# A linear-attention and token-mixing block: the whole last product by seven block products instead of three quarters of it, the first product in other groups

## The chip, the cores and the metric

One core of one Trainium2 chip. The metric is the time of one execution in microseconds of device time; the median of several runs is given. A separate execution is taken with the hardware profiler, and its trace shows when each engine worked and on what.

## What is computed

The input is a prompt of S = 2048 tokens with D = 448 channels. A linear attention block and then a token-mixing MLP, both with adaptive layer norm from a condition vector, are added to it. The change lies in the second half:

```python
def _B_ref(x, w1, b1, w2, b2):
    h = _layernorm(x, axis=-1)                     # (B, S, D)
    u = jnp.einsum("bsd,sf->bdf", h, w1) + b1      # (B, D, F), F = 1792
    u = _gelu(u)
    y = jnp.einsum("bdf,fs->bds", u, w2) + b2      # (B, D, S)
    return y transposed to (B, S, D)

x = x + ga * _A_ref(h, A_wqkv, A_wo)
h = _layernorm(x, axis=-1) * (1 + cb) + sb
x = x + gb * _B_ref(h, B_w1, B_b1, B_w2, B_b2)
```

So there are two large products. The *first product* is u = w1ᵀ h: for each of 14 blocks of 128 values of f, a sum over 16 tiles of 128 tokens. The *last product* is y = w2ᵀ u: for each of 16 tiles of 128 tokens, a sum over the 14 blocks of f. All arrays are float32.

## The kernel before

**Precision.** A float32 operand is cut in two parts of the format `fp32r`: ScalarE copies it (the high part), VectorE subtracts that from it (the low part). `split` (lines 78 to 80) does both. A product of two operands is then three matmuls, high by high, high by low and low by high. `acc3` (lines 833 to 836) issues these three, each with 128 stationary columns and 448 moving ones, into one PSUM bank.

**The first product.** w1 is read in *pieces*, each one token tile by a group of n blocks of f. `W1G` (line 291) has the groups: f 0 to 3, 4 to 7, 8 to 11 and then 12 and 13, so there are 64 pieces, of 512 columns or, in the last group, of 256. `load_to` issues their loads on SP's queue, `split_to` cuts them, `step` multiplies a piece with the normalised tokens `H2h`, `H2l` into n banks `up`. A group goes over all 16 token tiles, and then its n banks hold finished sums. Part of the first 20 pieces' work runs under the attention; from about 230 us on TensorE does nothing but the first product. In the loop over groups, each step also does: loads eight pieces ahead (`AHEAD`), cuts three ahead, one *job* out of a list, and at every second step one of the 16 x rows (the residual, to which the bias is added on VectorE, and which is then written to `out`, or to a parking place in DRAM for tiles 12 to 15).

**u and its parts.** `finish_u` (line 936) gives the jobs for one block f: gelu on ScalarE and a multiplication by the gate on VectorE; `cut`, the cut of the whole 448-wide u into `uw`, which holds the high part of both channel halves and then the low part of both; and, at each odd f, four sums and differences of the halves (`sums`) and their cuts `ut` (`parts4`).

**The last product by block products.** Two token tiles by two neighbouring blocks of f form a 2x2 block matrix a11, a12, a21, a22 of w2, and the two blocks of u, cut in two channel halves of 224, form another, b11 to b22. Seven products instead of eight then do, after Winograd's form of Strassen's scheme (`PRODS`, line 1005, gives for each of the seven the factor from w2, the factor from u, the bank it adds to, and the sum computed for a later one):

```python
    PRODS = (("a11", "b11", 0, None), ("a12", "b21", 1, ("s2", "s1", "a11")),
             ("s2", "t2", 0, ("s3", "a22", "s2", ALU.subtract, "a11")),
             ("s1", "t1", 2, ("s4", "a12", "s2", ALU.subtract, "a12")), ("s3", "t3", 0, None),
             ("s4", "b22", 2, None), ("a22", "t4", 0, None))
```

They are numbered m = 0 to 6; `q` numbers the pair of token tiles. `mult7` issues a product: for each of the seven pairs of f (`PAIRS`) one matmul of 448 moving columns, the high part of the factor from w2 by high and low part of the factor from u, and one of 224, its low part by the high part. For b11, b21 and b22 the moving operand is taken out of `uw`: 224 columns from the high part and 224 from the low part, which there lie 448 apart. For t1 to t4 both lie next to each other. `load_quads` loads the four blocks for all f in two DMAs each (four pairs of f, then three), and GpSimd's DMA adds a22 to a21, which makes s1. `split7` cuts one factor and computes the sum that `PRODS` names. `out7` takes a bank out: copies on ScalarE after m = 0, 2 and 3, sums on VectorE after m = 1, 4 and 5 (`out2`, two instructions each), both after m = 6. A finished tile `yt` is added to `out` in DRAM by GpSimd's DMA (`add_to_x`).

**The rest of the last product.** Token tiles 0 to 11 go this way (`NS7` = 6 pairs). Tiles 12 to 15 go the plain way: `load1`, `split1`, `mult1` with `acc3`, one *item* per f (two tiles at once for 12 and 13). The list `order` begins with eight plain items, mixes the others between the block products and ends with ten. The last two f of tile 15 are multiplied by `mult_last` in two halves of 224 columns, so that the first half is added and stored while the second is multiplied.

**What sets the order.** The order on every engine is that of the program: each engine's queue is strictly in turn, and there is no scheduler. A tile of SBUF comes from the pool `slots` (74 of 2 KB per partition); a new one waits until the one that had its place was read for the last time. SP's queue issues the plain loads and stores, GpSimd's the adding ones. Loads are issued 12 entries of `order` ahead (`LOAD2`), cuts four ahead (`SPLIT2`).

Of the kernel before, what the change touches and what calls it, by code (L numbers as in the profile page):

```python
# [33 lines left out]
AHEAD = 8  # L34
LAG = 5
LAST, CUT = 2, 224
# [11 lines left out]
def block_kernel(ctx: ExitStack, tc: tile.TileContext, x, xt, wqkv, wo, w1, b1, w2, b2, c, wmod, wfirst, out):  # L48
# [242 lines left out]
    W1G = [(0, 4), (4, 4), (8, 4), (12, 2)]  # L291
    pieces = [(w1, t, f0, n) for f0, n in W1G for t in range(NT)]
# [3 lines left out]
    def load_to(i):  # L296
        while done["load"] < min(i, len(pieces)):
            k = done["load"]
            src, r, c0, n = pieces[k]
            raws[k] = slot(f"pr{k}", n * P)  # L300
            nc.sync.dma_start(raws[k], src[r * P:(r + 1) * P, c0 * P:(c0 + n) * P])
            done["load"] += 1

    def split_to(i):
        while done["split"] < min(i, len(pieces)):
            k = done["split"]
            n = pieces[k][3]
            if k in TOKP:
                hi, lo = tslot(f"ph{k}", F32R, w=n * P), tslot(f"pl{k}", F32R, w=n * P)
            else:  # L310
                hi, lo = slot(f"ph{k}", n * P, F32R), slot(f"pl{k}", n * P, F32R)
# [526 lines left out]
    def step(k, accs, mh, ml, first, last):  # L838
        hi, lo = parts.pop(k)
        for i, ps in enumerate(accs):  # L840
            acc3(ps, hi, lo, slice(i * P, (i + 1) * P), mh, ml, first, last)
# [14 lines left out]
    for i in range(NT + LAG):  # L856
# [15 lines left out]
        if t >= 0:  # L872
            if t == 0:
                accs = [bank(f"up{f}") for f in range(4)]
            if i > NT:
                if not early:
                    early = [bank(f"up{W1G[1][0] + f}") for f in range(W1G[1][1])]
                r = i - NT - 1
                step(NT + r, early, H2h[r], H2l[r], r == 0, False)
            step(t, accs, H2h[t], H2l[t], t == 0, t == NT - 1)  # L880
# [55 lines left out]
    def finish_u(f, ps):  # L936
# [7 lines left out]
        def cut():  # L944
            uw[f] = uparts.tile([P, 4 * HD], F32R, name=f"uw{f}")
            split(ufull[f], uw[f][:, :D], uw[f][:, D:])
            w = uw[f].rearrange("p (x d) -> p x d", x=2)
            left, right = ((w[:, :, h:h + HD], w[:, 0, h:h + HD]) for h in (0, HD))
            if f % 2:
                uops["b21", r], uops["b22", r] = left, right  # L950
            else:
                uops["b11", r] = left
# [9 lines left out]
        def parts4(key, half, name):  # L962
            return lambda: u_parts(r, name, ufull[key][:, half * HD:(half + 1) * HD])
# [50 lines left out]
    def mult7(q, m):  # L1014
        a, b, k, _ = PRODS[m]
        opens = m in (0, 1, 3)
# [3 lines left out]
        closes = m in (1, 5, 6)  # L1020
        cut = hilo.pop((q, m))
        for r in range(PAIRS):
# [28 lines left out]
    def out7(q, m):  # L1051
# [20 lines left out]

    def load1(t, n, f):
        raw2[t, f] = slot(f"q{t}_{f}", n * P)
        nc.sync.dma_start(raw2[t, f], w2[f * P:(f + 1) * P, t * P:(t + n) * P])

    def split1(t, n, f):
        w = slot(f"qw{t}_{f}", 2 * n * P, F32R)
        hilo[t, n, f] = (w[:, :n * P], w[:, n * P:])
        split(raw2.pop((t, f)), *hilo[t, n, f])  # L1080

    def mult1(t, n, f):
        if f == 0:
            for i in range(n):
                acc2[t + i] = bank(f"yp{t + i}")
        hi, lo = hilo.pop((t, n, f))
        for i in range(n):
            acc3(acc2[t + i], hi, lo, slice(i * P, (i + 1) * P), uw[f][:, :D], uw[f][:, D:], f == 0,
                 f == NF - 1 - (LAST if t == NT - 1 else 0))


    def mult_last(t):
        nc.vector.tensor_add(X[t], acc2[t][:, :D], X[t])
        for c0, c1 in ((0, CUT), (CUT, D)):
            ps = bank(f"yl{c0}")[:, :c1 - c0]
            n = 0
            for f in range(NF - LAST, NF):
                wh, wl = hilo[t, 1, f]
                a, b = uw[f][:, c0:c1], uw[f][:, D + c0:D + c1]
                for w, m in ((wh, a), (wh, b), (wl, a)):  # L1100
                    nc.tensor.matmul(ps, w, m, start=n == 0, stop=n == 3 * LAST - 1)
                    n += 1
            x = X[t][:, c0:c1]
            nc.vector.tensor_add(x, ps, x)
            nc.sync.dma_start(of[t * P:(t + 1) * P, c0:c1], x)

    def out1(t, n, f):
        if f < NF - 1:
            return
        for i in range(t, t + n):  # L1110
            nc.vector.tensor_add(X[i], acc2[i][:, :D], X[i])
            store(i)


    sevens = [(q, m) for q in range(NS7) for m in range(7)]
    plains = [(t, n, f) for t, n in ((12, 2), (14, 1), (15, 1)) for f in range(NF)]
    LEAD, TAIL = 8, 10
# [152 lines left out]
```

## Time and profile before

| | us |
|---|---|
| median of 3 runs | 447.32 |
| lowest and highest | 446.92, 447.51 |
| the profiled execution | 448.35 |
| its span | 446.2 |

The span is the time from the first to the last recorded event of the profiled execution; the execution's own time has another 2.15 us around it. The page of the profile has the span in 40 slices. These are its rows for TensorE (PE), VectorE (DVE), ScalarE (ACT) and GpSimd (POOL); each digit is a slice's busy share in tenths:

```profile
PE   7999999999999999999999999999999999999997
PEld 6878899999899999989999999999999999999996
DVE  3989997689998899896477776649688787978873
ACT  3899877748656876667664345336554546356531
POOL 3227563300025355554300000000110211302101
```

A slice is 11.2 us. The first product alone has slices 21 to 28, the last product 29 to 40. In the last product the fourth row (ScalarE) stands at about half, the third (VectorE) at seven to nine tenths. In the rows of groups that the prediction shows, a line begins with the line of the code, the engine and the operation, then output and inputs by the program's names and their shapes; a row of a timeline begins with start and duration in us, and ends in brackets with the idle time before it and what ended it.

### The profile page before, as it was taken

What the parts mean: (1) busy time and instruction counts of PE and PEld (TensorE: products, weight loads), DVE (VectorE), ACT (ScalarE), POOL (GpSimd) and SP (SyncE); (2) the same over time, 40 slices, a digit from 0 to 9 for tenths busy, and PEclk for the clock granted to TensorE, in tenths of its full rate; (3) what the DMA queues carried; (4) which work ended last, traced back from release to release, by engine and by line L of the source; (5) the groups of instructions that cost most, each with busy time, mean ns of one, the idle gap of its engine ahead of it and who ended that gap; (6) DMA issues with size and microseconds to landing.
All of it is one profiled execution on the core that took longest, in us unless ns stands there. A gap on an engine that the chain in (4) does not pass through costs nothing.

```text
span 446.2 us, 7331 instructions
## 1 busy us (share of the span) xinstructions
PE 439.1 (98%) x2370; PEld 405.5 (91%) x2370; DVE 353.5 (79%) x801; ACT 267.5 (60%) x580; POOL 104.3 (23%) x188
## 2 busy tenths in 40 slices
PE   7999999999999999999999999999999999999997
PEld 6878899999899999989999999999999999999996
DVE  3989997689998899896477776649688787978873
ACT  3899877748656876667664345336554546356531
POOL 3227563300025355554300000000110211302101
PEclk9999999999999999999999999999999999999999
DMA  7997999545100004222416453227987569966334
GB/s 236 378 303 165 215 241 229 104 147 181 54 0 1 24 25 114 54 48 47 143 54 217 137 178 127 90 88 228 257 201 194 92 177 214 208 183 110 54 89 62
DMA packets 58853, 63.22 MB, mean 142 GB/s; under 512 B 5248, under 2 KB 49344, under 8 KB 58816
## 3 DMA queue, kind: packets, MB, share of 16 engines
q1 hardware_dynamic: 51616, 51.17, 38.0%
q0 software_dynamic: 7200, 11.60, 16.4%
q8 instruction: 18, 0.29, 0.3%
q14 instruction: 19, 0.16, 0.1%
HBM read 46.57 MB, written 7.34 MB: 121 GB/s over the span
## 4 chain that ended last, share of the span: by engine, by line
PE 91%; ACT 3%; DVE 2%; POOL 1%; DMA 1%; issue 1%; SPq 0%; ACTq 0%
PE y L1026 14%; PE up L836 10%; PE up L835 10%; PE up L834 9%; PE cacc L512 7%; PE qp L418 7%; PE op L783 7%; PE y L1027 7%; PE kp L418 6%; PE yp L834 2%; PE yp L836 2%; PE yp L835 2%; PE tq L767 1%; DMA xt<-in_xt_dram 1%; PE qp L425 1%
## 5 line engine op out<-in xcount | busy, mean ns | idle before, releaser
L836 PE MATMUL up<-h2h,pl 128*128 128x448 f32 x224 | 81.4, 363 | 0.0
L835 PE MATMUL up<-h2l,ph 128*128 128x448 f32 x224 | 81.2, 362 | 0.0
L834 PE MATMUL up<-h2h,ph 128*128 128x448 f32 x224 | 80.8, 361 | 0.0
L80 DVE TENSOR_TENSOR pl<-pr,ph 128x512 fp32r<-128x512 f32 (+1 forms) x60 | 36.3, 616 | 14.2 <-ACT ph L79 9.9
L79 ACT ACTIVATE ph<-pr 128x512 fp32r<-128x512 f32 (+1 forms) x60 | 33.0, 570 | 24.0 <-PE up L835 17.7
L835 PEld LDWEIGHTS up<-h2l,ph 128*128 128x128 f32 x224 | 42.1, 188 | 3.1
L834 PEld LDWEIGHTS up<-h2h,ph 128*128 128x128 f32 x224 | 41.9, 187 | 3.0
L836 PEld LDWEIGHTS up<-h2h,pl 128*128 128x128 f32 x224 | 42.1, 188 | 2.4
L988 POOL DMA_DIRECT2D a<-a x12 | 10.9, 952 | 113.8 <-DMA a<-in_B_w_dram 101.7
L1046 POOL DMA_DIRECT2D out_dram<-yt x12 | 10.5, 874 | 82.3 <-DVE yt L1037 53.9
L512 PE MATMUL cacc<-pkh,xh 128*128 128x448 f32 x64 | 24.4, 381 | 0.3 <-ACT pkh L486 0.3
L783 PE MATMUL op<-wph,pth 112*128 112x448 f32 x64 | 24.5, 382 | 0.0
L418 PE MATMUL kp<-wh,hh 128*128 128x448 f32 x64 | 23.2, 373 | 1.1 <-ACT wh L253 1.1
L1032 ACT ACTIVATE cc<-y 128x448 f32<-128x448 f32 x18 | 9.8, 545 | 23.4 <-PE y L1027 20.4
L512 PE MATMUL cacc<-pkl,xh 128*128 128x448 f32 x64 | 23.3, 364 | 0.2 <-DVE pkl L488 0.2
L418 PE MATMUL qp<-wh,hh 128*128 128x448 f32 x64 | 23.3, 364 | 0.0
L783 PE MATMUL op<-wpl,pth 112*128 112x448 f32 x64 | 23.2, 363 | 0.0
L783 PE MATMUL op<-wph,ptl 112*128 112x448 f32 x64 | 23.2, 362 | 0.0
L834 PE MATMUL yp<-uw,qw 128*128 128x448 f32 x54 | 19.9, 368 | 0.0
L771 ACT ACTIVATE pth<-tq 112x512 fp32r<-112x512 f32 x16 | 9.6, 599 | 17.1 <-PE tq L767 17.1
L836 PE MATMUL yp<-uw,qw 128*128 128x448 f32 x54 | 19.7, 364 | 0.0
L835 PE MATMUL yp<-uw,qw 128*128 128x448 f32 x54 | 19.6, 364 | 0.0
(241 smaller groups left out, 1308.9 us busy)
## 6 DMA issues: line engine op xcount, KB each, us to landing
pr<-in_B_w_dram SPq DMA_DIRECT2D x48, 256.0 KB, 3.0
a<-in_B_w_dram SPq DMA_DIRECT2D x24, 256.0 KB, 4.9
a<-in_B_w_dram SPq DMA_DIRECT2D x24, 192.0 KB, 4.9
xt<-in_xt_dram SPq DMA_DIRECT2D x16, 256.0 KB, 4.9
x<-in_A_x_dram SPq DMA_DIRECT2D x16, 224.0 KB, 4.9
wm<-in_B_wmod_dram SPq DMA_DIRECT2D x16, 196.0 KB, 5.1
wr<-in_qkv_dram SPq DMA_DIRECT2D x12, 224.0 KB, 5.3
out_dram<-x SPq DMA_DIRECT2D x12, 224.0 KB, 2.0
```

Source lines behind the costliest of these rows:

```text
L79: nc.scalar.activation(hi, full, AF.Copy)
L80: nc.vector.tensor_sub(lo, full, hi.bitcast(F32))
L418: nc.tensor.matmul(pps[t, j][:, :D], a[:, ch * P:(ch + 1) * P], w, start=first, stop=False)
L512: nc.tensor.matmul(cacc[ch][:, :D], a[:, s], b, start=(t == 0 and i == 0), stop=(t == NT - 1 and i == len(todo) - 1))
L783: nc.tensor.matmul(opb[t][:, :D], a[:, s], b, start=(n == 0), stop=(n == 11))
L834: nc.tensor.matmul(ps[:, :D], hi[:, sl], mh, start=first, stop=False)
L835: nc.tensor.matmul(ps[:, :D], hi[:, sl], ml, start=False, stop=False)
L836: nc.tensor.matmul(ps[:, :D], lo[:, sl], mh, start=False, stop=last)
L988: nc.gpsimd.dma_start(w, a, accum_op=ALU.add)
L1026: nc.tensor.matmul(ps[:, :D], h[:, s], w, start=opens and r == 0, stop=False, skip_group_check=True)
L1027: nc.tensor.matmul(ps[:, :HD], l[:, s], wh, start=False, stop=closes and r == PAIRS - 1, skip_group_check=True)
L1046: nc.gpsimd.dma_start(of[t * P:(t + 1) * P, :], ysum.pop(t), accum_op=ALU.add)
```

## The change

1. `NS7` is `NT // 2` = 8: all 16 token tiles go by block products. `load1`, `split1`, `mult1`, `out1`, `mult_last` and the mixed `order` go.
2. Every half of u that is a factor gets a tile of its own with high and low part next to each other: b11 of an even f, b21 and b22 of an odd one. The right half of an even f is no longer cut. These tiles, and the sums' cuts of the last two pairs of f (`UT_APART`), come from `uparts` instead of `slots`.
3. `mult7` takes a range of pairs. Five products are begun with six of the seven pairs (`BEGUN`), (q, m) = (0,0), (0,1), (0,3), (1,0), (1,1); then each gets its seventh; then the other products of q = 0 and 1 follow, mixed, and from q = 2 on m = 0 to 6 in turn.
4. `W1G` has groups of 4, 4, 2, 2 and 2 f. A piece of the groups of 2 f is two token tiles by two f, so that every piece has 512 columns and there are 56. `AHEAD` is 8 for the groups of four and `NEAR` = 5 for those of two; cuts are three or two ahead.
5. The x rows go at every step instead of every second one; all but tile 15 are written to `out` at once. `add_to_x` then serves 15 tiles.
6. Tile 15 is held in SBUF at the end (`fetch_x`) and is added to and stored in two halves by `finish`.
7. `PRE2` says after which token tiles of the last group loads and cuts for the last product are issued: five factors with their sums are cut there. `JOBS` and `CUT2` do the same for the first entries of `order`.

```diff
+AHEAD, NEAR = 8, 5
+PRE2 = ((0, (1, 0)), (6, (1, 1)), (8, (4, 2)), (12, (4, 3)), (14, (4, 4)), (15, (4, 5)))
+JOBS = {0: 2, 1: 2}
+UT_APART = 5
+CUT2 = {2: 9, 3: 9, 4: 8, 5: 7}
...
-    W1G = [(0, 4), (4, 4), (8, 4), (12, 2)]
-    pieces = [(w1, t, f0, n) for f0, n in W1G for t in range(NT)]
+    W1G = [(0, 4), (4, 4), (8, 2), (10, 2), (12, 2)]
+    pieces = [(t, 4 // n, f0, n) for f0, n in W1G for t in range(0, NT, 4 // n)]
+    place = {(f0, t + i): (k, i * n * P) for k, (t, m, f0, n) in enumerate(pieces) for i in range(m)}
...
-    NS7 = 6
-    uw, uops, ufull = {}, {}, {}
+    NS7 = NT // 2
+    uops, ufull = {}, {}
 
     def u_parts(r, name, src):
-        w = slot(f"u{name}_{r}", dt=F32R)
+        if name[0] == "b" or r >= UT_APART:
+            w = uparts.tile([P, D], F32R, name=f"u{name}_{r}")
+        else:
+            w = slot(f"u{name}_{r}", dt=F32R)
         split(src, w[:, :HD], w[:, HD:])
         uops[name, r] = (w, w[:, :HD])
...
-        def cut():
-            uw[f] = uparts.tile([P, 4 * HD], F32R, name=f"uw{f}")
-            split(ufull[f], uw[f][:, :D], uw[f][:, D:])
-            w = uw[f].rearrange("p (x d) -> p x d", x=2)
-            left, right = ((w[:, :, h:h + HD], w[:, 0, h:h + HD]) for h in (0, HD))
...
+        def part(key, half, name):
+            return lambda: u_parts(r, name, ufull[key][:, half * HD:(half + 1) * HD])
...
         if f % 2 == 0:
-            return [act, cut]
+            return [act, part(f, 0, "b11")]
         two = lambda p, q: lambda: (p(), q())
-        return [act, cut, sums, two(parts4(("a", r), 1, "t2"), parts4(("a", r), 0, "t1")),
-                two(parts4(("b", r), 0, "t3"), parts4(("b", r), 1, "t4"))]
+        return [act, two(part(f, 0, "b21"), part(f, 1, "b22")), sums,
+                two(part(("a", r), 1, "t2"), part(("a", r), 0, "t1")),
+                two(part(("b", r), 0, "t3"), part(("b", r), 1, "t4"))]
...
-    def mult7(q, m):
+    def mult7(q, m, r0, r1):
         a, b, k, _ = PRODS[m]
-        opens = m in (0, 1, 3)
+        opens = m in (0, 1, 3) and r0 == 0
...
-        closes = m in (1, 5, 6)
-        cut = hilo.pop((q, m))
-        for r in range(PAIRS):
+        closes = m in (1, 5, 6) and r1 == PAIRS
+        cut = hilo[q, m]
+        for r in range(r0, r1):
...
             out2(q, 0, "c5", t1, 1)
+            if q == NS7 - 1:
+                finish(t1, HD, yt(t1)[:, HD:])
         elif m == 5:
             out2(q, 2, "c2", t0, 1)
             add_to_x(t0)
+        elif q == NS7 - 1:
+            x = X[t1][:, :HD]
+            nc.vector.tensor_add(x, acc2[q, 0][:, :HD], x)
+            finish(t1, 0, acc2[q, 0][:, HD:D])
...
+    def finish(t, c0, y):
+        x = X[t][:, c0:c0 + HD]
+        nc.vector.tensor_add(x, y, x)
+        nc.sync.dma_start(of[t * P:(t + 1) * P, c0:c0 + HD], x)
...
+    FIRST = ((0, 0), (0, 1), (0, 3), (1, 0), (1, 1))
+    BEGUN = PAIRS - 1
+    order = [(q, m, 0, BEGUN) for q, m in FIRST]
+    order += [(q, m, BEGUN, PAIRS) for q, m in ((0, 0), (1, 0), (0, 1), (1, 1), (0, 3))]
+    order += [(q, m, 0, PAIRS) for q, m in ((0, 2), (1, 3), (0, 4), (0, 5), (1, 2), (0, 6), (1, 4), (1, 5), (1, 6))]
+    order += [(q, m, 0, PAIRS) for q in range(2, NS7) for m in range(7)]
...
-            load_to(k + AHEAD)
-            split_to(k + 3)
+            k = place[o0, r][0]
+            load_to(k + (AHEAD if n == 4 else NEAR))
+            split_to(k + (3 if n == 4 else 2))
             if jobs:
                 jobs.pop(0)()
-            if xleft and k % 2:
+            if xleft:
...
+            if o0 + n == NF:
+                for at, (load, cut) in PRE2:
+                    if at == r:
+                        load2(load)
+                        split2(cut)
```

More of the change, by code (lines that the diff above doesn't have):

```diff
@@ L1092, in mult_last @@
[L1092 to L1117, printed above, removed]
-    order = [("p", p) for p in plains[:LEAD]]
-    mid = plains[LEAD:len(plains) - TAIL]
-    for i, p in enumerate(sevens):
-        order.append(("s", p))
-        order += [("p", x) for x in mid[i * len(mid) // len(sevens):(i + 1) * len(mid) // len(sevens)]]
@@ L1133, in load2 @@
         while cnt["load"] < min(n, len(order)):
-            kind, p = order[cnt["load"]]
-            if kind == "p":
-                load1(*p)
-            elif p[1] == 0:
-                load_quads(p[0])
+            q, m, r0, _ = order[cnt["load"]]
+            if m == 0 and r0 == 0:
+                load_quads(q)
             cnt["load"] += 1
@@ L1145, in block_kernel @@
     xleft = list(range(NT))
-    xpark = {t: park.tile([P, D], F32, name=f"xpark{t}") for t in range(2 * NS7, NT)}
+    xpark = {t: park.tile([P, D], F32, name=f"xpark{t}") for t in range(NT - 1, NT)}
     stored = []
```

99 lines of the change are left out of this document (33 added, 66 removed).

## The prediction

> **What bounds the kernel now.** I read the page first (share of the span per engine), then what TensorE waited for, then the stretches by stage, then the order of time inside the last product.
>
> ```profile
> PE 439.1 (98%) x2370; PEld 405.5 (91%) x2370; DVE 353.5 (79%) x801; ACT 267.5 (60%) x580; POOL 104.3 (23%) x188
> ```
>
> TensorE (PE) is busy 98% of the span. Its waits are seven rows, of which these are the first and the last:
>
> ```profile
> PE warm L178 <- DVE roots L101: 1.1, 1, 1.1
> ...
> PE cacc L512 <- DVE pkl L488: 0.2, 1, 0.2
> ```
>
> Together the seven make 3.6 us, and none of them names `up`, `y` or `yp`, the tiles of the two products that the change touches. So there TensorE's own work is the time. The stretches say the same; the columns are length, then busy time of PE, weight load, VectorE (DVE), ScalarE (ACT), GpSimd (POOL), clock, DMA share and GB/s:
>
> ```profile
> 230.00:316.10 86.10, 86.10 (x433) 80.71 (x432) 60.29 (x138) 39.37 (x89) 0.00 (x0) 1.00 0.51 158
> 325.60:436.10 110.50, 110.50 (x677) 104.44 (x676) 90.75 (x187) 55.09 (x128) 18.48 (x21) 1.00 0.66 148
> ...
> 443.04:446.20 3.16, 0.00 (x0) 0.00 (x0) 0.39 (x1) 0.00 (x0) 0.00 (x0) 1.00 0.21 73
> ```
>
> The granted clock is 1.00 in all. In the second VectorE is at 82%: the engine to watch. The last product runs from the first start of `yp` to the end of the chain:
>
> ```profile
> L834 PE MATMUL yp<-uw,qw x54: 360/363/381, 316.1 to 440.9; 128*128 128x448 f32 x54
> ```
> ```profile
> 441.70 1.34 PE yl L1101 x12
> 443.04 0.02 issue
> 443.07 0.39 DVE xb L1104
> ```
>
> That is 443.04 - 316.1 = 126.9 us of TensorE; the 3.16 us of the third stretch, to the span's end at 446.2, lie behind its last matmul.
>
> **TensorE, part by part.** The price of a step is the distance between starts, not the printed duration (matmuls overlap):
>
> ```profile
> 365.08 0.36 PE L1026 MATMUL y<-uw,a11h 128*128 128x448 f32 x1
> ...
> 367.31 0.38 PE L1026 MATMUL y<-uw,a12h 128*128 128x448 f32 x1
> ...
> 369.55 0.38 PE L834 MATMUL yp<-uw,qw 128*128 128x448 f32 x1
> ...
> 370.18 0.36 PE L1026 MATMUL y<-ut,s2h 128*128 128x448 f32 x1
> ...
> 372.36 0.38 PE L1026 MATMUL y<-ut,s1h 128*128 128x448 f32 x1
> ```
>
> A block product (seven pairs of one 448-wide and one 224-wide matmul) takes 2.23 to 2.24 us when its moving operand is `uw`, whose two halves are read across a gap, and 2.18 us with `ut`, which lies in one piece. A plain item (three 448-wide matmuls) took 0.63 us here.
> Before: 18 products with `uw` (40.2), 24 with `ut` (52.3), 12 half-wide matmuls of the last tile (1.34), which leaves 126.9 - 93.8 = 33.1 us for 54 plain items, 0.61 each, as the row has it. After: 56 products, all with an operand in one piece: 56 x 2.18 = 122.1, and 0.16 for the last matmul's drain (0.27 long, 0.11 apart). So TensorE's stage gives **-4.7 us**: -3.9 from 34.4 us of plain work replaced by 14 products (30.5), -1.0 from the 18 products that lose the gap, +0.2 drain. Bounds: -3.7 if the 2.23 comes from something other than the gap, for those 18, and 24 x 0.055 = 1.3 less (-3.4) if it also holds for the new ones; -5.2 if the 0.63 of an item between products is what each of them cost.
> The Trainium skill, "TensorE: Matmul & The Clock Gate", section "Wait — 56ns, not 53.3ns?", has starts N / 2.4 GHz + 2.5 ns apart, 189 and 96 ns here, whether the operand has a gap or not. By it a product would be 1.99 us and an item 0.57, and the stage would give -3.9 us as an estimate. The rows above have an item at 0.63 and two layouts apart, so they decide.
>
> The first product keeps its 672 matmuls; in groups of 2 f each step has six instead of twelve, and a load brings two token tiles. TensorE's price there is nothing as long as pieces come in time: VectorE has 70% of 230 to 316 us to do. The x rows now go at every step. That adds no instruction, only packs 16 of them, and a step of twelve matmuls (2.4 us) holds a piece, a job and an x. I take 0, from 0 to +0.5.
>
> **VectorE in the last product.** It cuts and sums for all 8 pairs of tiles. Distance between starts:
>
> ```profile
> 384.45 1.15 DVE L80 TENSOR_TENSOR s2l<-s,s2h 128x512 fp32r<-128x512 f32 x2
> 385.52 1.15 DVE L994 TENSOR_TENSOR a<-a,s 128x512 f32<-128x512 f32 x2
> ...
> 388.73 0.61 DVE L1036 TENSOR_TENSOR cc<-y,cc 128x448 f32<-128x448 f32 x1
> 389.38 0.39 DVE L1037 TENSOR_TENSOR yt<-cc 128x224 f32<-128x224 f32 x1
> 389.69 0.28 DVE L80 TENSOR_TENSOR qw<-q,qw 128x128 fp32r<-128x128 f32 x1
> ```
>
> Per pair: ten halves-of-seven-blocks operations at 1.07 (7 low parts, s2, s3, s4), three outputs at 0.96, one half-wide addition at 0.31 (0.39 printed, 389.38 to 389.69): 13.9 us, against TensorE's 7 x 2.18 = 15.3. That is 91%, where it was 82% with 18.6 us a pair. It still fits, and cuts are made four products ahead (8.7 us). The tightest place is m=4: its sum must be read before m=6 adds to the same bank, 2.18 us later; VectorE needs 0.65 for it and comes to it with the low part of the next a11 just done. ScalarE cuts at 0.94 a block:
>
> ```profile
> 393.37 1.03 ACT L79 ACTIVATE a22h<-a 128x512 fp32r<-128x512 f32 x2
> 394.31 0.30 ACT L79 ACTIVATE qw<-q 128x128 fp32r<-128x128 f32 x1
> ```
>
> Seven of those and four copies (at most 0.55 each) are 8.8 of 15.3. I take 0.
>
> **The join.** Let T be the end of the first product. Five products are begun without f = 12, 13: 30 pairs, 9.4 us of cover. VectorE's queue then holds, in program order: s2 of q=1, u12, its b11, u13, b21 and b22, four sums, s2's low part and s3 of q=0, t2, t1, s1's low part and s4 of q=1, t3, t4, two outputs, s3's low part.
>
> ```profile
> 240.83 0.62 DVE L942 TENSOR_TENSOR u<-u,mod 128x448 f32<-128x448 f32 x1
> 241.37 0.68 DVE L1179 SCALAR_TENSOR_TENSOR x<-mod,b2c,x 128x448 f32<-128x448 f32 x1
> ```
>
> From u12: 2 x 0.54, 11 halves at 0.31, four blocks at 1.07, two outputs at 0.96, 0.6 for the first part of s3, and some 1.6 for ScalarE's turns between them make 12.9 us. If u12 starts at T + 0.3 (behind its gelu), s3 is there at T + 13.2; TensorE wants it (q=0, m=4) after 30 + 5 pairs and two products, at T + 10.9 + 4.4 = T + 15.3. So **2.1 us of slack**. It is eaten by s2 of q=1, which stands ahead of u12 and waits for a DMA that adds a22 to a21:
>
> ```profile
> a<-in_B_w_dram SPq DMA_DIRECT2D x24, 256.0 KB, 4.9
> ```
> ```profile
> a<-a POOLq DMA_DIRECT2D x6, 256.0 KB, 4.5
> ```
> ```profile
> 338.06 4.72 SPq L983 DMA_DIRECT2D a<-in_B_w_dram  x8
> ```
>
> The eight loads of q=1 go into buffers of pieces read at token tiles 5 and 6 of the last group (each 1.2 us), so from T - 12.2. Issued over 4.7 us and landing 4.9 after issue, the last is there at T - 2.6, the adding DMA at T + 1.9 to T + 2.8 (its two issues stand 0.9 apart), s2 done 0.5 later. u12 is then up to 3 us late against 2.1 of slack. I take **+0.3 us**, from 0 to +1.5. Without the five begun products TensorE would stand still for most of the 9.4 us. What is late next, s4 and s2 of q=1, has as much or more slack, as TensorE is put back by the same stall.
>
> **The end.** Before, the last addition ended at 443.07 + 0.39 = 443.46 and the span 2.74 later.
>
> ```profile
> 434.17 0.40 DVE L1037 TENSOR_TENSOR yt<-cc 128x224 f32<-128x224 f32 x1
> ```
> ```profile
> 434.97 0.87 POOL L1046 DMA_DIRECT2D out_dram<-yt  x1 [13.53 <-DVE qw L80]
> ```
> ```profile
> out_dram<-yt POOLq DMA_DIRECT2D x2, 224.0 KB, 3.9
> ```
> ```profile
> out_dram<-xb SPq DMA_DIRECT2D x2, 112.0 KB, 1.7
> ```
>
> After TensorE's end E there are two dependent additions (0.39 + 0.04 + 0.39) and a store by SP, so the end is E + 0.03 + 0.82 + 2.74 = E + 3.6. But tile 14 now goes out by an adding DMA behind m=5, which ends at E - 2.18: 1.05 for its output, 0.40 to GpSimd's issue, 3.9 to landing, E + 3.2; with what lies behind a landing (2.74 - 1.7 = 1.0) E + 4.2. Against 3.16 that is **+1.0 us**, from +0.4 (SP's store is last) to +1.6 (4.5 to landing).
>
> Sum: 446.2 - 4.7 + 0.3 + 1.0 = 442.8, or -3.4. The profiled execution took 448.35 us (2.15 around its span), the median of the timed runs is 447.32; -3.4 from that is **443.9**.
>
> **Rivals.**
> *The join stalls for real.* If GpSimd's adding DMA takes the 6.6 us that one took below, and VectorE enters T with a piece or two behind it, u12 is 5 us late and the stall 3 us.
>
> ```profile
> a<-a POOLq DMA_DIRECT2D x2, 192.0 KB, 6.6
> ```
>
> For it: that row, VectorE's strict order. Against: no other load is under way at that time. 443.9 + 2.7 = 446.6.
> *VectorE becomes the bound (slower).* If its operations cost what is printed (1.15 + 0.08 for a block whose two parts overlap by 0.08) and not 1.07, and it waits for ScalarE once a pair as it does here,
>
> ```profile
> 391.57 1.16 DVE L80 TENSOR_TENSOR s4l<-a,s4h 128x512 fp32r<-128x512 f32 x2 [0.53 <-ACT s4h L79]
> ```
>
> a pair is 12.3 + 3.0 + 0.4 + 0.5 = 16.2 us, over TensorE's 15.3. From 15.3 on it sets the pace: 8 x 0.9 = 7.2, so 443.9 + 7.2 = 451.1. For it: 91%, and the wait. Against: the starts 1.07 apart, and that ScalarE was late there through a copy that itself waited for TensorE, which falls away when VectorE is the late one.
> *The gap isn't what made `uw` slow:* the bound above, -3.4 in place of -4.7: 443.9 + 1.3 = 445.2.
> *Weight loads set the pace (slower).* PEld is busy 104.44 of 110.5, 0.154 each; after there are 784 loads for 762, so +3.4 in place of -4.7: 447.32 + 3.4 + 1.3 = 452.0. Against: twelve half-wide matmuls with a load each took 1.34, 0.112 each. The Trainium skill, "Perfetto Trace Analysis", section "Identifying the Most-Contended Engine", would judge TensorE by just this share; by that rule it is full. The 0.112 speaks against it, and the chance is small.
>
> **Chances.** Forecast 0.74; join 0.10 (half of it still faster by over 0.2%); VectorE 0.07; gap 0.07; weight loads 0.02. 0.2%, or 0.9 us, is about what a measurement of this kernel tells from no change. Faster 0.74 + 0.07 + 0.05 = 0.86, slower 0.09, same 0.05. The range goes from 442.5 (-5.2 + 0.4) to 446.3 (a stall of some 2.5 us).
>
> **What would show it.** Right: TensorE without a wait at the join or one of under a microsecond; products 2.18 apart whatever the operand; last product near 122.3 us; VectorE near 90% in it; the last landing GpSimd's. Wrong: rows of TensorE's waits that name `y` with s2, s3 or `cc` as releaser; VectorE without idle time; pieces `pl` late in the groups of 2 f; products with b11 at 2.23.

## The result and the profile after

| | before, us | after, us |
|---|---|---|
| median of 6 runs each | 447.31 | 445.22 |
| lowest and highest | 446.56, 448.34 | 444.60, 445.59 |
| the profiled execution | 448.35 | 445.22 |
| its span | 446.2 | 443.5 |

The changed kernel is faster by 2.1 us: after to before 0.9954, 95% interval 0.9944 to 0.9965. The forecast was 443.9, so the sign is right and the gain is 1.3 us smaller than forecast. All rows that follow are read for those 1.3 us.

The busy shares, and what TensorE waited for (us in total, times, longest), after the change; of the six rows of waits, 2.3 us together, these are the first and the last:

```profile
PE 436.6 (98%) x2392; PEld 404.4 (91%) x2392; DVE 364.7 (82%) x811; ACT 273.3 (62%) x572; POOL 110.0 (25%) x195
```
```profile
PE warm L181 <- DVE roots L104: 1.1, 1, 1.1
...
PE tq L769 <- DVE pn L758: 0.2, 1, 0.2
```

None of the six names `y` or `up`: nothing in the two products waits, at the join neither. So TensorE's price and the tail behind it are all there is to explain. Two stretches after, by busy time of each engine (60 us out of the last product, then the whole of it), and the end of the chain that finished last among the engines:

```profile
340.00:400.00 60.00, 60.00 (x383) 57.20 (x382) 55.41 (x108) 33.82 (x71) 15.00 (x17) 1.00 0.87 188
...
315.48:439.00 123.52, 123.49 (x785) 117.48 (x783) 109.33 (x218) 67.43 (x142) 23.60 (x27) 1.00 0.67 143
```
```profile
438.87 0.11 PE y L1025
...
439.43 0.39 DVE xb L1078
```

TensorE's last product takes 438.98 - 315.48 = 123.50 us, where it took 126.94: -3.44, not the -4.7 of the sum. The tail from there to the span's end is 443.5 - 438.98 = 4.52 us, where it was 3.16: +1.36, not +1.0. These two give -2.1, which is the timed difference. The span fell by another 0.6 because the first product ended at 315.48 and not at 316.1; as far as single executions can tell, that isn't the change's: it ended at 315.52 in another execution with the first product of before (e11 below), and between 314.9 and 315.9 in the executions below with that of after or with its groups undone.

The start of a product, and of the next one, after the change (start, printed duration, engine, line, tiles):

```profile
370.53 0.38 PE L1024 MATMUL y<-ut,s3h 128*128 128x448 f32 x1
...
372.72 0.38 PE L1024 MATMUL y<-ub,s4h 128*128 128x448 f32 x1
...
374.93 0.38 PE L1024 MATMUL y<-ut,a22h 128*128 128x448 f32 x1
...
377.13 0.38 PE L1024 MATMUL y<-ub,a11h 128*128 128x448 f32 x1
...
379.34 0.38 PE L1024 MATMUL y<-ub,a12h 128*128 128x448 f32 x1
```

Every operand lies in one piece now, and still no product costs 2.18: 2.19 and 2.20 with `ut`, 2.21 with `ub`. So either the gap wasn't what cost, or the 2.18 was no product's own price. That is what the first experiments ask.

### The profile page after: what moved, and what is told of

The parts are those of the page before. It is cut to its first block, busy times and chain, and to the rows that moved or that the text cites. A ratio compares the mean times of both kernels' runs of the same rounds, so it can differ in the third digit from the quotient of the medians.

```text
span 443.5 us, 7249 instructions
## 1 busy us (share of the span) xinstructions
PE 436.6 (98%) x2392; PEld 404.4 (91%) x2392; DVE 364.7 (82%) x811; ACT 273.3 (62%) x572; POOL 110.0 (25%) x195
## 4 chain that ended last, share of the span: by engine, by line
PE 93%; ACT 3%; DVE 2%; POOL 1%; issue 1%; ACTq 0%
PE y L1024 19%; PE up L838 10%; PE up L837 10%; PE up L836 9%; PE y L1025 9%; PE cacc L514 7%; PE qp L420 7%; PE op L785 7%; PE kp L420 6%; PE tq L769 1%; PE col L218 1%; PE warm L181 1%; PE qp L427 1%; PE kvb L725 1%; PE rowb L283 1%; PE wp L853 1%
## 5 line engine op out<-in xcount | busy, mean ns | idle before, releaser
L986 POOL DMA_DIRECT2D a<-a x16 | 14.1, 960 | 142.7 <-DVE u L950 76.9
L83 DVE TENSOR_TENSOR pl<-pr,ph 128x512 fp32r<-128x512 f32 x52 | 34.6, 686 | 3.1 <-ACT ph L82 2.3
L82 ACT ACTIVATE ph<-pr 128x512 fp32r<-128x512 f32 x52 | 31.2, 626 | 3.3 <-PE up L837 2.6
L1030 ACT ACTIVATE cc<-y 128x448 f32<-128x448 f32 x24 | 12.9, 544 | 23.7 <-PE y L1025 23.7
L1044 POOL DMA_DIRECT2D out_dram<-yt x15 | 13.6, 908 | 48.6 <-DVE yt L1035 38.1
L950 DVE TENSOR_TENSOR u<-u,mod 128x448 f32<-128x448 f32 x14 | 8.7, 621 | 18.8 <-ACT u L949 18.6
L949 ACT ACTIVATE u<-up,b1c 128x448 f32<-128x448 f32 x14 | 8.7, 624 | 23.9 <-PE up L838 21.9
L827 ACT ACTIVATE y<-y,nb,rt 128x448 f32<-128x448 f32 x16 | 12.1, 758 | 11.8 <-POOL nb L826 11.8
```

Of the source, the lines that this page charges most:

```text
L82: nc.scalar.activation(hi, full, AF.Copy)
L83: nc.vector.tensor_sub(lo, full, hi.bitcast(F32))
L986: nc.gpsimd.dma_start(w, a, accum_op=ALU.add)
L1044: nc.gpsimd.dma_start(of[t * P:(t + 1) * P, :], ysum.pop(t), accum_op=ALU.add)
```

## The experiments

Unless it is said otherwise, each is the changed kernel with one edit. "Timed" means five rounds beside the kernel before (three in e1); the others are one execution with its trace. The total of one kernel differs by 1 us and more from one execution to the next; the length of its last product doesn't: it is 123.5 us in the changed kernel and in e3 and e7, where TensorE does the same.

**e1: the gap back in b11, b21, b22.**

```diff
         if name[0] == "b" or r >= UT_APART:
+            if name == "b11":
+                w = uparts.tile([P, 3 * HD], F32R, name=f"u{name}_{r}")
+                split(src, w[:, :HD], w[:, D:])
+                uops[name, r] = (w.rearrange("p (x d) -> p x d", x=3)[:, 0:3:2, :], w[:, :HD])
+                return
...
```

(b21 and b22 share one tile, as `uw` was laid out.)

> The changed kernel, but the two halves of b11, b21 and b22 lie with a gap of 896 bytes between them again, cut as before (the same instructions of ScalarE and VectorE). In the changed kernel a product with ub takes 2.21 us and one with ut 2.20, not the 2.18 of the prediction. Theory 1 (the gap costs something, but the 2.18 that the prediction took for a product without it contained a first pair of 0.30 behind a plain item, and every other pair costs 0.314): the 24 products with b11, b21 and b22 go from 2.21 to 2.23 or 2.24, the whole from 445.2 to 445.8, and products with ut stay at 2.20. Theory 2 (the gap costs nothing; the 2.24 of before came from the plain items between the products): they stay at 2.21 and the time at 445.2. Theory 3 (the prediction's 0.055 a product): from 2.21 to 2.26, +1.3 us, 446.5.

A product whose operand is read across the gap, and the next one's start, in e1:

```profile
379.18 0.38 PE L1037 MATMUL y<-uw,a12h 128*128 128x448 f32 x1
...
381.40 0.37 PE L1037 MATMUL y<-ut,s2h 128*128 128x448 f32 x1
```

2.22 here; over all whole products 2.21 to 2.22 with the gap, 2.20 to 2.21 with `ut`. The last product took 438.95 - 315.16 = 123.8 us (+0.3), and the timed median is 445.22, ratio 0.9953 (0.9936 to 0.9970), that of the changed kernel. In this layout the gap is worth 0.01 us a product at most, and the prediction's 0.055 falls as a price of the gap as such. The run isn't clean: a tile of three halves is 2688 bytes, no multiple of 256, so the parts of u no longer start at the same byte of 256, and the start has a price of its own (e5, e6 and e9).

**e4: in each product all matmuls of 448 first, then those of 224.** Perhaps a 448-wide matmul behind a 224-wide one is what costs.

```diff
             nc.tensor.matmul(ps[:, :D], h[:, s], w, start=opens and r == 0, stop=False, skip_group_check=True)
+        for r in range(r0, r1):
+            (h, l), i = cut[r // 4], r % 4
+            w, wh = uops[b, r]
+            s = slice(i * P, (i + 1) * P)
             nc.tensor.matmul(ps[:, :HD], l[:, s], wh, start=False, stop=closes and r == PAIRS - 1,
```

> The changed kernel, but in each product the 448-wide matmuls of all pairs run first and the 224-wide ones behind them, so that a 448-wide one follows a 448-wide one. Theory 1 (a matmul of 448 costs 0.200 behind another one and 0.212 behind one of 224, in which the next weights aren't loaded yet; one of 224 costs 0.10 to 0.112): a product takes 7 x 0.20 + 7 x 0.11 = 2.17 to 2.18, which gives 56 x 0.025 = 1.4 us, 443.8. Theory 2 (it is a price of each matmul whatever stands ahead of it): 2.20 as now, 445.2. Theory 3 (weight loads, 0.154 busy each, set the pace where narrow matmuls follow one another): 7 x 0.20 + 7 x 0.154 = 2.48, +15 us.

In its order of time the seven of each width now stand together, so each has its own price:

```profile
342.03 1.58 PE L1024 MATMUL y<-ub,s4h 128*128 128x448 f32 x7
343.45 0.94 PE L1029 MATMUL y<-ub,s4l 128*128 128x224 f32 x7
344.22 1.60 PE L1024 MATMUL y<-ut,a22h 128*128 128x448 f32 x7
```

Seven of 448 take 1.42 us (0.203 each), seven of 224 take 0.77 (0.110 each), together 2.18 to 2.21, as when mixed. The last product is 438.96 - 315.64 = 123.3 us, the timed median 445.31, ratio 0.9950 (0.9937 to 0.9963). The order changes nothing in the sum (theory 2), and weight loads set no pace (theory 3). Of theory 1 the first half is right: by the distance between starts, in e4 and in the changed kernel, a matmul of 448 takes 0.20 us behind another of 448 and 0.21 behind one of 224. But one of 224 takes 0.10 behind one of 448 and 0.11 behind another, so a product pays the same either way. From the two prices: (0.203 - 0.110) / 224 is 0.415 ns a column, and 0.203 less 448 of these leaves 0.017 us for each matmul, whatever its width. With 0.203 and 0.110 the last product before (456 matmuls of 448 and 306 of 224) and after (392 and 392) differ by -64 x 0.203 + 86 x 0.110 = -3.5 us; -3.4 was measured.

In the kernel before, this moves time from a product to its neighbour. The start of the product with s2 that the prediction shows, which stands behind a plain item:

```profile
370.18 0.36 PE L1026 MATMUL y<-ut,s2h 128*128 128x448 f32 x1
370.38 0.27 PE L1027 MATMUL y<-ut,s2l 128*128 128x224 f32 x1
370.48 0.38 PE L1026 MATMUL y<-ut,s2h 128*128 128x448 f32 x1
370.69 0.27 PE L1027 MATMUL y<-ut,s2l 128*128 128x224 f32 x1
```

Its first matmul of 448 follows one of 448 and takes 0.20 us, the next follows one of 224 and takes 0.21. Of the 24 products with `ut`, 18 stood like this and took 2.183 on average; the six behind another product took 2.192. A plain item behind a product paid it back, with 0.62 to 0.63 us where items in a row took 0.60. So the 2.18 was in part the neighbour's: the 0.63 that the prediction noticed is the other side of it.

**e5, e6, e9: where the parts of u start.** What is left between `ub` and `ut` is where they start in a partition, counted within 256 bytes. Parts from `uparts` (`uw` before; `ub`, and the `ut` of the last two pairs, after) start at byte 192, the `ut` in `slots` at byte 128. In e6, `moving` gives a slot's row 64 bytes further on.

```diff
e5, all at 128:
-    uspace.tile([P, 16], F32, name="uspace")
+    uspace.tile([P, 64], F32, name="uspace")
e6, all at 192:
-            w = slot(f"u{name}_{r}", dt=F32R)
+            w = moving(slot, f"u{name}_{r}")
e9, all at 0:
-    uspace.tile([P, 16], F32, name="uspace")
+    uspace.tile([P, 32], F32, name="uspace")
...
-            w = slot(f"u{name}_{r}", dt=F32R)
+            w = slot(f"u{name}_{r}", 512, F32R)[:, 32:32 + D]
```

> The changed kernel, with one padding tile made 192 bytes longer, so that the parts of u in the pool of their own start at the same byte of 256 (128) as those in the shared slots; in the changed kernel they start at 192, and those in the slots at 128. Theory 1 (a matmul costs its width over the clock and a constant, 0.204 us for 448 and 0.111 for 224, whatever it reads and in whatever order): products with ub stay at 2.20 to 2.21, the last product at 123.3 to 123.5 us. Theory 2 (the start within 256 bytes sets the 0.01 between ub at 2.21 and ut at 2.20): products with ub go to 2.20, the last product to 123.2 or less. Theory 3 (it also was what made 2.24 and 2.18 of uw and ut before): to 2.18, the last product to 122.3.

> The changed kernel, with the parts of u in the shared slots moved up by 64 bytes, to byte 192 of 256, where those in the pool of their own start. Theory 1 (width and a constant alone): 2.20 to 2.21 for all, last product 123.3 to 123.5 us. Theory 2 (the start sets it): ut at 2.21 as ub, last product 123.8. Theory 3: ut at 2.23 to 2.24, last product 124.9.

> The changed kernel with all parts of u starting at byte 0 of 256 (at 128 a product took 2.194 us and the last product 123.0; at 192 2.209 and 123.85). Theory 1 (what counts is how many stretches of 256 bytes a row of 1792 bytes touches: 7 from byte 0, 8 from 64, 128 and 192, while the 896 bytes of the narrow one touch 4, 4, 4 and 5): below 2.19, the last product under 122.8. Theory 2 (stretches of 128 bytes: 14 and 7 from 0 as from 128, 15 and 8 from 64 and 192): 2.194 and 123.0, as at 128. Theory 3 (the start has nothing to do with it, and the two runs differ by chance): anything between 2.19 and 2.21.

Five successive products of e5, then of e6, then of e9, from the first start to the start behind the last:

```profile
374.26 0.37 PE L1024 MATMUL y<-ut,a22h 128*128 128x448 f32 x1
...
385.23 0.38 PE L1024 MATMUL y<-ut,s3h 128*128 128x448 f32 x1
```
```profile
375.48 0.38 PE L1024 MATMUL y<-ut,a22h 128*128 128x448 f32 x1
...
386.52 0.38 PE L1024 MATMUL y<-ut,s3h 128*128 128x448 f32 x1
```
```profile
375.25 0.37 PE L1024 MATMUL y<-ut,a22h 128*128 128x448 f32 x1
...
386.34 0.37 PE L1024 MATMUL y<-ut,s3h 128*128 128x448 f32 x1
```

10.97, 11.04 and 11.09 us for five: 2.194 a product from byte 128, 2.208 from 192, 2.218 from 0, and within a run `ub` and `ut` cost the same. The last product was 123.0, 123.8 and 124.3 us. The 123.0 came again in e12 below. So the start within 256 bytes does matter (e5's and e6's theory 2), but by 0.02 us; e9's two counting rules, by which 0 is as good as 128 or better, both fall. By what rule the start counts stays open; 64 for all wasn't tried.

**e11: the kernel before, with `uw` at byte 128,** the gap left in. The edit is that of e5.

> The kernel before, with the padding tile 192 bytes longer, so that uw starts at byte 128 of 256, not 192; the gap between its halves stays. Before, products with uw took 2.218 to 2.240 us and those with ut 2.180 to 2.190, 42 of them 92.5 us together, the 54 plain items 33.1. Theory 1 (start and gap are worth 0.015 and 0.01 at most, the rest of the difference is how the plain items between them are counted): uw products go down by about 0.015, the last product from 126.9 to 126.4 or 126.6. Theory 2 (the start made most of it): uw products to 2.18 to 2.20, the last product to 126.0. Theory 3 (neither): 126.9 as it was.

Two products like those in the prediction's rows, 2.23 and 2.24 there:

```profile
382.31 0.37 PE L1026 MATMUL y<-uw,a11h 128*128 128x448 f32 x1
384.50 0.38 PE L1026 MATMUL y<-uw,a12h 128*128 128x448 f32 x1
...
386.69 0.37 PE L834 MATMUL yp<-uw,qw 128*128 128x448 f32 x1
```

2.19 each, like those with `ut`, although the halves still lie apart. Over all 42 products those with `uw` went from a mean of 2.226 to 2.197 and those with `ut` rose from 2.185 to 2.194; the mean of all went from 2.202 to 2.196 and the last product from 126.9 to 442.13 - 315.52 = 126.6. So by the products with `uw` theory 2 holds, by the sum theory 1, because those with `ut` rose; why they did wasn't found. The plain items stayed within 0.1 us of their 33.

The products with a11 and a12, whose operand now starts at byte 128, took 2.191 and 2.195, as e5's do without a gap. Those with s4 read the right half, which lies 896 bytes further on and so starts at byte 0; they took 2.206. From byte 128 the gap costs nothing, then. From 192 that is open: a product with a12 took 2.240 before, with the gap, and 2.209 after, without it, both from 192 and behind one with a11, and no run changes the gap alone there.

What matters here is that 2.202 is also the mean of the 56 products after the change, and e5's is 2.193 where e11's is 2.196. **A product's mean price was the same in both kernels, whether its halves lay apart or not.** The rows of 2.18 that the prediction took for the price were one operand's, shortened by the plain items ahead of them.

**e3: tile 14 without the adding DMA.** Its rows are fetched back like tile 15's and SP stores the halves.

```diff
-            add_to_x(t0)
+            if q == NS7 - 1:
+                finish(t0, HD, yt(t0)[:, HD:])
+            else:
+                add_to_x(t0)
...
```

> The changed kernel, but tile 14 isn't added by GpSimd's DMA to rows that lie in the output: its rows are fetched back as tile 15's are, two additions of VectorE (0.31 each) bring them in, and SP stores both halves. Theory 1 (the end is the landing of that adding DMA): the tail behind the last matmul goes from 4.5 to 3.6 us, the span down by 0.9, the time to 444.3. Theory 2 (SP's last store lands as late, or what lies behind a landing is longer): 445.0 to 445.3. Theory 3: the two additions come before the low parts that the last products need, and TensorE waits 0.3 to 0.6 for them; then 444.6 to 444.9.

The tail in e3 as a stretch, and what its last two stores took from issue to landing (the last number, in us); then, in the changed kernel, the issues of the adding DMA and of SP's last store and what each took from issue to landing:

```profile
438.53:442.40 3.87, 0.00 (x0) 0.00 (x0) 0.78 (x2) 0.00 (x0) 0.00 (x0) 1.00 0.17 59
```
```profile
out_dram<-xb SPq DMA_DIRECT2D x2, 112.0 KB, 1.7
```
```profile
438.27 0.88 POOL L1044 DMA_DIRECT2D out_dram<-yt  x1 [11.22 <-DVE yt L1035]
...
439.85 0.34 SPq L1079 DMA_DIRECT2D out_dram<-xb  x1
```
```profile
out_dram<-yt POOLq DMA_DIRECT2D x1, 224.0 KB, 3.9
out_dram<-xb SPq DMA_DIRECT2D x1, 112.0 KB, 2.6
```

3.9 us for 4.5. The timed median is 444.62, ratio 0.9939 (0.9926 to 0.9951), 0.6 below the changed kernel. The adding DMA lengthened the tail, but not as theory 1 has it: it landed at 438.27 + 3.9 = 442.2, and SP's store at 439.85 + 2.6 = 442.5, so the store was last in the changed kernel too. It took 2.5 to 2.7 us in all ten traces with the adding DMA under way and 1.7 in the two without (e3 and e12): that is 1.0 less in e3. The gain is only 0.6, because in e3 the span ends at 442.4, which is 1.3 us behind that landing (439.40 + 1.7 = 441.1) and not 1.0; why is open.

**e2: the first five products whole, none begun.**

```diff
...
-    order = [(q, m, 0, BEGUN) for q, m in FIRST]
-    order += [(q, m, BEGUN, PAIRS) for q, m in ((0, 0), (1, 0), (0, 1), (1, 1), (0, 3))]
+    order = [(q, m, 0, PAIRS) for q, m in FIRST]
...
```

(`JOBS` and `CUT2` are set anew, so that the last f's parts of u are made in the same order, save for one output of VectorE ahead of the sums.)

> The changed kernel, but the first five products run whole, without being begun on six of seven pairs first; the last f's parts of u are made in the same order, save that one output of VectorE stands ahead of the sums. Theory of the prediction: TensorE stands still for most of the 9.4 us that the thirty begun pairs cover, say 6 to 9 us. Theory from the trace of the changed kernel (u12 ready 2.9 us behind the end of the first product, its b11 3.8, b21 and b22 5.7, t1 about 9): the first product meets its last pair at 1.9 us and waits 1.9, the second is in time, the third waits about 0.9; 2 to 3 us in all, as all that is behind it can run under the other products. The time is then 447.2 to 448.2.

TensorE's two new waits, the stretches behind the first of them (the last four columns: GpSimd, granted clock, DMA share, GB/s), and the starts of the pair that waited and of the seventh after it:

```profile
PE y L1024 <- DVE ub L83: 2.5, 1, 2.5
PE y L1024 <- DVE x L1122: 1.2, 1, 1.2
```
```profile
320.00:322.00 2.00, 2.00 (x8) 1.85 (x9) 0.20 (x1) 1.07 (x2) 0.00 (x0) 0.61 1.21 290
322.00:324.00 2.00, 2.00 (x9) 1.87 (x8) 1.11 (x3) 0.67 (x2) 0.00 (x0) 0.54 0.80 191
324.00:326.00 2.00, 2.00 (x15) 1.88 (x13) 1.53 (x4) 0.00 (x0) 1.76 (x2) 1.00 0.25 43
```
```profile
320.00 0.48 PE L1024 MATMUL y<-ub,a11h 128*128 128x448 f32 x1 [2.52 <-DVE ub L83]
...
323.89 0.37 PE L1024 MATMUL y<-ub,a12h 128*128 128x448 f32 x1
```

The time is 450.94 and the span 449.2, 5.7 more. Only 3.7 of that are waits, in the two places that the trace had named. Behind the wait of 2.5 us the clock fell to about half, and eight or nine matmuls went through in 2 us where 15 do at full speed: the seven pairs from 320.00 to 323.89 took 3.89 us for 2.20, 1.7 us more. The remaining 0.3 us lie in the two pairs with the waits in them, which took 2.7 and 1.4 us longer than others, for waits of 2.5 and 1.2. Behind the other wait, of 1.2 us, the clock stayed at 1.00.

The Trainium skill, "TensorE: Matmul & The Clock Gate", section "Why this matters for your kernels", allows idle gaps of up to about 3 us before the clock drops to half. That the drop is to half agrees with the 0.54 here; the gap that brought it was 2.5 us, which is shorter.

**e8: the first product in groups of 4, 4, 4, 2 again.**

```diff
-    W1G = [(0, 4), (4, 4), (8, 2), (10, 2), (12, 2)]
+    W1G = [(0, 4), (4, 4), (8, 4), (12, 2)]
```

> The changed kernel with the first product in groups of 4, 4, 4, 2 f as before, the rest as it is (x rows at every step, the same begun products). Theory 1 (the prediction: TensorE does the same 672 matmuls and no piece is late, so groups of 2 cost and bring 0): 445.2, within 0.3. Theory 2 (groups of 2 are what brings the jobs of f = 8 to 11 out early; with a group of 4 those of 8 to 11 stand in the last group, with the pieces, the x rows and the cuts of the first products, and VectorE comes late to the join): TensorE waits 1 to 3 us there, 446.2 to 448.2, more if its clock drops behind the wait as it did for 3.3 us (to 0.54 to 0.61) without the begun products.

Timed 445.31, ratio 0.9956 (0.9943 to 0.9970); TensorE's waits are the six of the changed kernel, and the last product took 438.79 - 314.92 = 123.9 us, 0.4 more than now. That lies in a single place: the first pair of the first product with s3 took 331.01 - 330.32 = 0.69 us for 0.31, at the join where s3 is barely in time as it is. In the time of the whole, the groups alone bring nothing that can be measured.

**e7 and e10: two and four more operations of VectorE for each pair of tiles.**

```diff
             split(w, h, l)
             hilo[q, m].append((h, l))
+        if m in (0, 4):
+            nc.vector.tensor_sub(more, more, more)
```

(in e10 m = 0, 2, 4, 6)

> The changed kernel with two more 128x512 subtractions of VectorE for each pair of tiles (in the cuts of a11 and s3), on a tile of their own that nothing else reads; they add 2 x 0.6 = 1.2 us to the 13.9 of a pair, 15.1 of 15.4 (98%), from 92%. Theory 1 (VectorE has the 8% to give; TensorE sets the pace): at the join, where s3 came 0.35 us before it was needed, one such operation puts it 0.25 to 0.9 us behind, and nothing else waits; span 443.8 to 444.4. Theory 2 (VectorE's strict order, with its waits for ScalarE, makes a pair longer than the sum of its work, so the margin is smaller than 8%): waits of TensorE for low parts in many pairs, 0.3 to 0.8 us a pair, span 446 to 449.

> The changed kernel with four more 128x512 subtractions of VectorE for each pair of tiles (cuts of a11, s2, s3, a22), on a tile of their own; with two of them VectorE was busy 99% and TensorE waited for nothing. Four add 2.4 us: 16.3 of 15.4. Theory 1 (VectorE sets the pace from 15.4 on): TensorE waits some 0.9 us a pair from the join on, 5 to 7 us in all, span 448.5 to 450.5. Theory 2 (each such wait also lowers TensorE's clock, as the wait of 2.5 us did without the begun products): more than the waits by 1 us and over, span 451 to 460.

The same 60 us of e7 and of e10, and the one wait for VectorE that e10's rows add in the last product:

```profile
340.00:400.00 60.00, 60.00 (x383) 57.15 (x383) 59.34 (x115) 33.55 (x70) 15.65 (x18) 1.00 0.86 188
```
```profile
340.00:400.00 60.00, 56.74 (x356) 53.10 (x355) 59.59 (x115) 30.38 (x64) 14.55 (x17) 1.00 0.80 171
```
```profile
PE y L1028 <- DVE cc L1038: 5.0, 7, 1.5
```

With two, VectorE is busy 99% and TensorE waits for nothing in the product: the span is 443.8, the last product 123.5. With four, VectorE sets the pace: the span is 450.7, 7.2 more, with the clock at 1.00 throughout. The wait is the one that the prediction called the tightest place, the output of m=4 that m=6 must wait for. It comes seven times, at most 1.5 us long, and the clock holds.

**e12: put together.** Tile 14 as in e3, the parts of u at byte 128 as in e5, and in the last product of all the seven narrow matmuls behind the wide ones, in a bank of their own, so that two of three additions run under them.

```diff
...
+            nc.vector.tensor_add(x, acc2[q, 0][:, HD:D], x)
             nc.vector.tensor_add(x, acc2[q, 0][:, :HD], x)
-            finish(t1, 0, acc2[q, 0][:, HD:D])
+            ps = bank("yl")[:, :HD]
+            for r in range(PAIRS):
+                l, i = hilo[q, m][r // 4][1], r % 4
+                nc.tensor.matmul(ps, l[:, i * P:(i + 1) * P], uops["t4", r][1], start=r == 0, stop=r == PAIRS - 1)
+            finish(t1, 0, ps)
...
```

> The changed kernel with tile 14 stored from SBUF by SP (as without the adding DMA at the end), all parts of u starting at byte 128 of 256, and in the very last product the 448-wide matmuls first, then the 224-wide ones into a bank of their own, so that two of three additions run under the latter. Theory: 445.2 less 0.6 (tile 14), less 0.5 (last product 123.5 to 123.0), less 0.4 (one addition of 0.39 behind the last matmul in place of two): 443.7, tail 3.5 us in place of 4.5. Rivals: the landing behind SP's last store takes what it wants and the third step brings 0: 444.1; the start of u's parts is run-to-run chance and brings 0: 444.2; both: 444.6.

Its end, as the order of time and as a stretch:

```profile
437.67 0.94 PE L1081 MATMUL yl<-ut,a22l 128*128 128x224 f32 x7
437.87 0.39 DVE L1076 TENSOR_TENSOR xb<-y,xb 128x224 f32<-128x224 f32 x1
...
438.79 0.39 DVE L1091 TENSOR_TENSOR xb<-yl,xb 128x224 f32<-128x224 f32 x1
```
```profile
438.61:442.20 3.59, 0.00 (x0) 0.00 (x0) 0.47 (x2) 0.00 (x0) 0.00 (x0) 1.00 0.19 64
```

443.90 timed, ratio to before 0.9922 (0.9909 to 0.9936), 1.3 us below the changed kernel. The last product is 438.61 - 315.62 = 123.0, as in e5, and the tail 3.6. It is faster than both kernels, and the steps add as their rows said: -0.5 from the start, -0.9 from the tail (443.7 was expected).

## Why the prediction was right, and where its gain was too large

*What bounds.* TensorE, before and after; its own price is the time. Right, and e7 says how firmly: VectorE can go to 99% before it costs.

*TensorE, -4.7 us: this is the term that was mis-sized, -3.4 measured.* Of its three parts the drain (+0.2) was right. The -3.9 for plain work replaced by 14 products was -3.6, since a product costs 2.202 and not 2.18 (34.4 - 14 x 2.202 = 3.6). The gap's -1.0 was 0 in the sum: the 18 products with `uw` became cheaper by 0.014 each (2.226 to 2.212 with `ub`), and the 24 with `ut` dearer by 0.011 (2.185 to 2.196). Both errors have one root: the difference between rows of 2.18 and 2.24 was read as a property of the operand's layout, and the lower one as what all would cost. The lower one came in part from the plain items ahead of it (e4), the higher one went away when `uw` started at another byte, though the gap stayed (e11); what the gap adds from byte 192 stays open. The total of before, 126.9 us, was explained as well by 42 products at their mean, 2.202. Of the signs that were named, products 2.18 apart and a last product near 122.3 us didn't come.

The rival "the gap isn't what made `uw` slow", to which the prediction gave 0.07 and 445.2 us, has the number, and its doubt was sound. Its prices are not what came: it kept 2.18 for `ut` and 0.055 more for the 24 products with halves of u, and the trace has 2.196 and 0.016 more. That the total comes out at 445.2 is also luck: the join brought 0.3 less and the end 0.4 more than in its sum.

*Weight loads.* The Trainium skill, "Perfetto Trace Analysis", section "Identifying the Most-Contended Engine", would judge TensorE by their busy share, and by that it was full. After the change they are busy 117.48 of 123.52 us, 95%, with more matmuls in less time; e4 ran seven narrow ones in a row at 0.110. The rival falls as argued. The Trainium skill, "TensorE: Matmul & The Clock Gate", section "Wait — 56ns, not 53.3ns?", gave -3.9 as an estimate, nearer than the rows as they were read: its price for a column agrees with e4 (0.415 ns measured), its constant of 2.5 ns doesn't (17 ns measured).

*The first product, 0.* Right: no piece late, and e8.

*VectorE at 91%, 0.* Right: 55.41 of 60 us, 92%, no wait. The price of its being the bound, 7.2 us for 0.9 us too much a pair, was right in size too, though what it took was four more operations (e10).

*The join, +0.3.* It was 0, but by little. VectorE's rows there, and the start of the product (q=0, m=4) that needs s3:

```profile
317.31 0.56 DVE L992 TENSOR_TENSOR s<-a,a 128x384 f32<-128x384 f32 x1 [0.51 <-DMA a<-a]
317.79 0.62 DVE L950 TENSOR_TENSOR u<-u,mod 128x448 f32<-128x448 f32 x1
...
329.85 1.16 DVE L83 TENSOR_TENSOR s3l<-a,s3h 128x512 fp32r<-128x512 f32 x2
...
330.89 0.38 PE L1024 MATMUL y<-ut,s3h 128*128 128x448 f32 x1
```

As worked out, s2 waited for the adding DMA and held u12 back, to T + 2.3 (T is the end of the first product) where it was to start at T + 0.3. That used up 2.0 of the 2.1 us of slack: s3's cut ends at 331.0, and its first part, which is read first, about half a microsecond earlier, before 330.89. What falls is the aside that without the begun products TensorE would stand still for most of 9.4 us: e2 shows 3.7 us of waits. But the edit is worth 5.7, since a wait there also costs clock.

*The end, +1.0.* +1.4, inside its bounds. The adding DMA went as worked out: it was issued 0.71 us before the last matmul's end E, where 0.73 was worked out (2.18 - 1.05 - 0.40), and landed 3.9 later, at E + 3.2. But the path was the other one: SP's store was taken at 1.7 us, took 2.6 beside the adding DMA and landed last, at E + 3.5, with 1.0 behind it. So the sign "the last landing GpSimd's" didn't come, and the size was near because the two landings lie 0.3 us apart.

## What to carry to other kernels

Where two groups of rows have the same work and prices a few per cent apart, check that the mean over all of them explains the stage before the difference is given to the one feature that one knows of; a run with that feature alone put back, and every other address in its place, settles it. A price read between two starts also depends on what stands ahead: read it behind different neighbours. On an engine that is full, the price of a regrouped product is its columns plus a constant for each instruction, and both follow from the rows of two widths. A tail is part of the change: here it gave back 1.4 of the 3.4 us, and of two transfers in flight the one that was issued last landed last, later than it would have alone.

## What the hardware showed that was not expected

The byte at which a row of 1792 bytes starts in SBUF changes a pair of matmuls by up to 1%: 2.194, 2.208 and 2.218 us a product from bytes 128, 192 and 0 of 256. Matmuls of 448 alone, in the plain items, went the other way where many stood in a row: the first 48 took 325.68 - 316.08 = 9.60 us from byte 192 (before) and 325.25 - 315.52 = 9.73 from 128 (e11). No rule was found.

A wait of 2.5 us was enough to halve TensorE's clock for over 3 us (e2); one of 1.2 us (e2) or seven of up to 1.5 us (e10) were not.

A plain store of 112 KB, issued 1.6 us behind an adding DMA of 224 KB, took 2.6 us to land; by itself it took 1.7.
